# Hash attention with a feed-forward block: key tiles in groups of two, queries and keys turned by VectorE, hashes on column halves of TensorE

## The chip, the cores and the metric

One core of a Trainium2 chip. The metric is the device time of one execution in microseconds (us), lower is better. All runs are of one core; the runs of one kernel in one job mostly agree within 0.3%. Engines are named as the profile does: PE is TensorE (PEld its weight loads), DVE VectorE, ACT ScalarE, POOL GpSimd, SP the queue that issues the DMAs.

## The reference, cut to what matters

```python
batch, n_heads, seq, head_dim = (4, 8, 768, 64)        # proj: 64 x 6
q_bucket = sum((q @ proj > 0) * 2**arange(6))          # k_bucket likewise
mask     = q_bucket[..., :, None] == k_bucket[..., None, :]
scores   = where(mask, q @ k.T / 8, -1e9)
attn     = softmax(scores);  x = attn @ v              # -> (3072, 512)
h = x @ w_in;  g = h * sigmoid(1.702 * h)              # w_in 512 x 2048
out = g @ w_out                                        # w_out 2048 x 512
```

The two weights arrive as 64-bit floats and are converted to 32-bit on the chip, in 16 chunks each.

## The kernel before

Work goes by 16 pairs of heads. A pair has 12 units: six key tiles (`kt`) for each of two query halves (`c`). Per unit TensorE makes two score matrices (one per head, each on 64 rows of the array, f32, with a bf16 part that adds a huge negative number where the hashes differ), ACT takes the exponential, DVE sums, and TensorE multiplies with v (one head on each 64-column half of the array). The preparation of the next pair is put between the units:

```python
def turned(c, ...):                         # 2 per tensor: three transposes on TensorE, copy on ACT
    for i in range(HT):
        nc.tensor.transpose(tp[:, i, :], x[:, c * HT + i]..., ident)
    nc.scalar.mul(xt[:, cols], tp, ...)

def hashed(c, ...):                         # 2 per tensor: a matmul on the whole array
    nc.tensor.matmul(dots, pb, xt[:, cols], start=True, stop=True)
    nc.vector.tensor_scalar(bits[:, cols], dots, ...)

def scores(n, c, kt):
    for a, m, last in ((kb, qb, False), (kT, qT, True)):        # bf16 first, then f32
        for j in range(2):
            nc.tensor.matmul(ps[:, j, 0:HS], a[hs, keys], m[hs, cols], start=not last, stop=last)
    nc.scalar.activation(es[c][:, kt, :, 0:HS], ps[:, :, 0:HS], Act.Exp)
# ... in the loop over units u:
    scores(*units[u]); sums(*units[u - 1]); values(*units[u - 2])   # plus total, invert, norm at a half's end
    todo.pop(0)()                                                   # one step of the next pair's preparation
```

In the feed-forward, `hidden(n)` makes 16 strips of h for 512 tokens (8 matmul passes each), `outputs(n)` the result. Inside the first 16 strips w_out is converted, a chunk per strip, with one set of buffers:

```python
    nc.scalar.activation(g[:, fc, :], h, Act.Gelu_apprx_sigmoid)
    if convs:
        for _ in convert(*convs.pop(0)):    # sign, bits, xor, sign, (ACT) size, scale, (POOL) add, scale
            pass
```

## Time and profile before

| | before |
|---|---|
| median of 3 runs | 1122.27 us (1120.23 to 1122.54) |
| span of the profiled run | 1120.4 us |
| attention, to the first feed-forward matmul | 448.2 us |
| one pair of heads in the steady part | 27.10 us |
| first feed-forward matmul to first output matmul (two `hidden`) | 116.4 us |
| all output matmuls and the other `hidden`, from first to last start | 548.9 us |

The pair is the distance between the first f32 score matmul of the second pair (42.09 us) and of the last (421.53), over 14. The profile's lines that carry the argument are in the prediction. Two habits are needed to read them. PE is "busy" for 98% of the span, but its recorded spans overlap where matmuls are pipelined, so what a matmul takes of the array is the distance from start to start. And an f32 matmul is recorded as two passes: "x4" of an f32 matmul are two instructions, one per head, of two passes.

### The profile page before, as it was taken

The page shows a single profiled execution, that of the slowest core. Times are in us where ns is not written, and L with a number is a line of the kernel's source. Part 1 is how long each engine was busy: PE and PEld are TensorE (multiplying, and loading weights), DVE is VectorE, ACT ScalarE, POOL GpSimd, SP SyncE. Part 2 cuts the span into 40 slices and gives each one's busy share as a digit, 9 for nine tenths or more (in the row PEclk, how much of TensorE's full clock was granted, in tenths as well). Part 3 has the DMA queues.
Part 4 walks back from the last instruction along what each step waited for, and adds up shares of the span by engine and source line. Part 5 has one row for each costly group of instructions (what it writes and reads, how often), then busy time and mean ns, then how long its engine had stood idle before and what let it go on. Part 6 is the DMA issues. An engine that isn't in the chain of part 4 may idle for free.

```text
span 1120.4 us, 9656 instructions
## 1 busy us (share of the span) xinstructions
PE 1099.1 (98%) x3905; PEld 451.1 (40%) x3905; DVE 368.3 (33%) x646; ACT 290.0 (26%) x450; POOL 51.1 (5%) x40
## 2 busy tenths in 40 slices
PE   6999999999999999998999999999999999999997
PEld 3333333333333333443444444444444444444443
DVE  2666666666666667565000000000000000000000
ACT  3555555445445554322100110011001100110000
POOL 0000000000100000222000000000000000000000
PEclk9999999999999999999999999999999999999999
DMA  5222222222222220231000000000000000000000
GB/s 122 62 62 61 62 62 62 61 62 62 64 68 72 62 61 20 93 114 57 1 9 19 9 1 9 19 9 1 9 19 9 1 19 19 0 1 19 19 19 21
DMA packets 83541, 42.65 MB, mean 38 GB/s; under 512 B 76320, under 2 KB 76320, under 8 KB 83488
## 3 DMA queue, kind: packets, MB, share of 16 engines
q1 hardware_dynamic: 83488, 41.96, 13.8%
q8 instruction: 32, 0.52, 0.2%
q14 instruction: 21, 0.17, 0.1%
HBM read 35.65 MB, written 6.29 MB: 37 GB/s over the span
## 4 chain that ended last, share of the span: by engine, by line
PE 92%; DVE 4%; POOL 2%; issue 1%; DMA 1%; ACT 0%; SPq 0%; ACTq 0%; DVEq 0%
PE y L411 29%; PE h L399 24%; PE ps L216 16%; PE av L236 14%; PE hash L172 5%; PE tp L165 3%; PE dn L243 2%; POOL w_out_sb L127 2%; DVE bits L118 1%; DVE w_out_sb L125 1%; DMA k<-in_k_dram 1%; DVE sign L121 1%; DVE sign L115 1%; DVE bits L116 0%; ACT L401 0%
## 5 line engine op out<-in xcount | busy, mean ns | idle before, releaser
L399 PE MATMUL h<-xT,w_in_sb 128*128 128x512 f32 x768 | 333.1, 595 | 4.2 <-ACT g L401 3.8
L411 PE MATMUL y<-w_out_sb,g 128*128 128x512 f32 x768 | 330.4, 592 | 0.0
L399 PEld LDWEIGHTS h<-xT,w_in_sb 128*128 128x128 f32 x768 | 146.1, 191 | 189.9 <-issue 181.4
L411 PEld LDWEIGHTS y<-w_out_sb,g 128*128 128x128 f32 x768 | 145.9, 190 | 183.7 <-issue 183.7
L414 DVE COPY o<-y 128x512 f32<-128x512 f32 x24 | 16.6, 693 | 571.5 <-PE y L411 571.5
L217 ACT ACTIVATE e<-ps 128x768 f32<-128x768 f32 x192 | 155.6, 810 | 173.5 <-PE ps L216 171.6
L401 ACT ACTIVATE g<-h 128x512 f32<-128x512 f32 x96 | 56.9, 596 | 439.8 <-PE h L399 439.8
L236 PE MATMUL av<-e,v 128*64 128x385 f32 x768 | 166.9, 514 | 0.0
L216 PE MATMUL ps<-qT,kT 64*128 64x384 f32 x768 | 155.8, 484 | 0.0
L229 DVE TENSOR_TENSOR acc<-acc,e 128x768 f32<-128x768 f32 x128 | 122.2, 954 | 15.6 <-ACT e L217 12.3
L236 PEld LDWEIGHTS av<-e,v 128*64 128x64 f32 x768 | 38.2, 135 | 104.7 <-issue 104.6
L216 PEld LDWEIGHTS ps<-qT,kT 64*128 64x128 f32 x768 | 69.8, 191 | 0.2 <-issue 0.2
L216 PE MATMUL ps<-qb,kb 64*128 64x384 bf16 x384 | 64.7, 333 | 0.3 <-DVE qb L175 0.3
L216 PEld LDWEIGHTS <-kb 64*128 64x128 bf16 x384 | 18.5, 92 | 85.7 <-issue 85.6
L127 POOL TENSOR_TENSOR w_in_sb<-bits,w_in_sb 128x512 f32<-128x512 f32 x16 | 30.0, 1875 | 404.5 <-DVE w_in_sb L125 404.5
L225 DVE SCALAR_TENSOR_TENSOR acc<-e 128x768 f32<-128x768 f32 x32 | 30.6, 955 | 24.5 <-ACT e L217 24.5
L173 DVE TENSOR_SCALAR qb<-hash,q_off 128x384 bf16<-128x384 f32 x32 | 19.1, 598 | 55.7 <-PE hash L172 55.7
L173 DVE TENSOR_SCALAR kb<-hash,k_off 128x384 bf16<-128x384 f32 x32 | 19.8, 618 | 44.5 <-PE hash L172 44.5
L123 ACT ACTIVATE size<-raw 128x512 f32<-128x512 f32 x32 | 21.5, 672 | 43.8 <-DVE w_out_sb L130 43.8
L172 PE MATMUL hash<-kT,pb 128*128 128x384 f32 x64 | 30.3, 560 | 0.0
L172 PE MATMUL hash<-qT,pb 128*128 128x384 f32 x64 | 29.0, 537 | 0.0
L243 PE MATMUL dn<-acc,ones 128*64 128x384 f32 x128 | 26.1, 487 | 0.0
(49 smaller groups left out, 359.0 us busy)
## 6 DMA issues: line engine op xcount, KB each, us to landing
raw<-in_moe_w_in_dram SPq DMA_DIRECT2D x16, 512.0 KB, 3.6
raw<-in_moe_w_out_dram SPq DMA_DIRECT2D x16, 512.0 KB, 3.3
k<-in_k_dram SPq DMA_DIRECT2D x32, 192.0 KB, 3.2
q<-in_q_dram SPq DMA_DIRECT2D x32, 192.0 KB, 3.8
v<-in_v_dram SPq DMA_DIRECT2D x32, 192.0 KB, 3.2
out_dram<-o SPq DMA_DIRECT2D x24, 256.0 KB, 2.0
pb<-in_proj_dram SPq DMA_DIRECT2D x2, 1.5 KB, 2.2
```

What stands on the lines that cost most here:

```text
L127: nc.gpsimd.tensor_tensor(dst, bits.bitcast(F32), dst, op=Alu.add)
L165: nc.tensor.transpose(tp[:, i, :], x[:, c * HT + i].rearrange("p j d -> p (j d)"), ident)
L172: nc.tensor.matmul(dots, pb, xt[:, cols], start=True, stop=True)
L173: nc.vector.tensor_scalar(bits[:, cols], dots, 0.0, off[:, 0:1], op0=op, op1=Alu.subtract)
L216: nc.tensor.matmul(ps[:, j, 0:HS], a[hs, keys], m[hs, cols], start=not last, stop=last)
L217: nc.scalar.activation(es[c][:, kt, :, 0:HS], ps[:, :, 0:HS], Act.Exp)
L229: nc.vector.tensor_tensor(acc, acc, e[:, kt, :, 0:HS], op=Alu.add)
L236: nc.tensor.matmul(av[D * j : D * (j + 1), :], vt[:, kt, j, :], es[c][:, kt, j, :], start=(kt == 0), stop=(kt == T - 1))
L243: nc.tensor.matmul(dn[D * j : D * (j + 1), :], ones, acc[:, j, :], start=True, stop=True)
L399: nc.tensor.matmul(h, w_in_sb[:, kc, fc * P : (fc + 1) * P], xT[:, kc, n * NT : (n + 1) * NT], start=(kc == 0), stop=(kc == KC - 1))
L401: nc.scalar.activation(g[:, fc, :], h, Act.Gelu_apprx_sigmoid)
L411: nc.tensor.matmul(y, g[:, fc, i * P : (i + 1) * P], w_out_sb[:, fc, :], start=(fc == 0), stop=(fc == FC - 1))
```

## The change

The intent is to take work off TensorE, which sets attention's pace: the transposes go to DVE (the DMA brings q and k in blocks of 32 columns, which DVE turns block by block), the hash of a tensor is made in one step on the two column halves of the array, next to matmuls of the same shape, and the array changes between scores and values once per two key tiles. Some of DVE's sums go to POOL, and the conversion of w_out is spread over two strips per chunk. The diff, cut to its core:

```diff
+            def turn(n, name):
+                x = raws.pop((n, name))
+                xt = xts[n, name] = wk.tile([P, S], F32, ...)
+                nc.vector.transpose(xt, x.rearrange("p s i -> p (s i)"))
+            def hashed(n, name):
+                for c in range(2):
+                    nc.tensor.matmul(h[D * c : D * (c + 1), :], pf[name], xts[n, name][:, c * HS : (c + 1) * HS],
+                                     start=True, stop=True)
+            def featured(n, name):
+                nc.vector.tensor_scalar(f, dots.pop((n, name)), above[name][:, 0:1], FEAT[name], ...)
+                ...                       # four small DMAs bring f to its place, as operand of the scores
             def scores(n, c, kt):
-                for a, m, last in ((kb, qb, False), (kT, qT, True)):
+                for a, m, last in ((kT, qT, False), (kf, qf, True)):
...
-            def sums(n, c, kt):
+            def add(n, c, kts):
+                    if kt in (1, 3):
+                        nc.gpsimd.tensor_tensor(acc, e[:, kt - 1, ...], e[:, kt, ...], op=Alu.add)
+                    elif kt == 5:         # on DVE: tiles 4 and 5, then the two partial sums
...
+            for g in range(len(groups) + 3):
+                    for i in range(2):
+                        scores(n, c, kt + i)
...
+                    add(pn, pc, (pkt, pkt + 1))
+                    for i in range(2):
+                        values(pn, pc, pkt + i)
...
-                    if convs:
-                        for _ in convert(*convs.pop(0)):
-                            pass
+                    next(steps, None)     # a chunk in two strips, two sets of buffers, next load issued ahead
```

Left out: the constants of the hash, the loads and stores in the tokens' natural order, the second path for large inputs, which does not run here, and its threshold, and the scale of 1/8, which moves from the copies on ACT into the exponential.

More of the change, by code (lines that the diff above doesn't have):

```diff
@@ L24 @@
 BIT = 2.0**33
-SAFE, SAFE_BITS = 64.0, 0x42800000
+FEAT = {"q": 2.0**16, "k": -(2.0**16)}
+NORMAL = 2.0**-126
+SAFE, SAFE_BITS = 32.0, 0x42000000
 TINY = 2.0**-100
@@ L65 @@
     HS = HT * P
-    assert D == 64 and S == 2 * HS and HS < 512 and HP == KC and DM <= 512 and NB < 32
+    assert D == 64 and S == 2 * HS and HS < 512 and HP == KC and DM <= 512 and 2 * NB <= 32
     const = ctx.enter_context(tc.tile_pool(name="const", bufs=1))
@@ L91 @@
     k_off = offsets("k_off", -NB / 2.0)
+    pf, above = {}, {}
+    for x, signs in (("q", (1.0, -1.0)), ("k", (-1.0, 1.0))):
+        w = pf[x] = const.tile([P, D], F32, name=f"pf_{x}")
+        nc.vector.memset(w, 0.0)
+        th = above[x] = const.tile([P, 1], F32, name=f"above_{x}")
+        nc.vector.memset(th, 0.0)
+        for j in range(2):
+            rows = slice(D * j, D * (j + 1))
+            for i, sign in enumerate(signs):
+                c0 = 32 * j + NB * i
+                nc.vector.tensor_scalar(w[rows, c0 : c0 + NB], pb[rows, D * j : D * j + NB], sign, None, op0=Alu.mult)
+            for c in range(2):
+                r0 = D * c + 32 * j
+                nc.vector.memset(th[r0 : r0 + 2 * NB], 0.0 if signs[1] > 0 else -NORMAL)
+                nc.vector.memset(th[r0 : r0 + NB], 0.0 if signs[0] > 0 else -NORMAL)
     xT = const.tile([P, KC, N], F32, name="xT")
@@ L101, with convert @@
     CW = 512
-    cv = ctx.enter_context(tc.tile_pool(name="cv", bufs=1))
-    def convert(dst, src):
-        raw = cv.tile([P, CW, 2], U32, tag="raw", name="raw", bufs=2)
+    def convert(cv, dst, src):
+        raw = cv.tile([P, CW, 2], U32, tag="raw", name="raw")
         nc.sync.dma_start(out=raw, in_=src)
@@ L144, in load @@
             for j in range(2):
-                nc.sync.dma_start(out=x[:, :, j, :], in_=src[b, 2 * hp + j].rearrange("(p t) d -> p t d", p=P))
+                nc.sync.dma_start(out=x[:, :, j, :], in_=src[b, 2 * hp + j].rearrange("(t p) d -> p t d", p=P))
             tiles[name] = x
@@ L183, in attention @@
         with actx:
-            ld = actx.enter_context(tc.tile_pool(name="ld", bufs=2))
+            ld = actx.enter_context(tc.tile_pool(name="ld", bufs=1))
             wk = actx.enter_context(tc.tile_pool(name="wk", bufs=2))
             ep = actx.enter_context(tc.tile_pool(name="ep", bufs=1))
+            cv = actx.enter_context(tc.tile_pool(name="cv", bufs=1))
             st = actx.enter_context(tc.tile_pool(name="st", bufs=2))
@@ L195, in attention @@
                 nc.gpsimd.memset(e[:, :, :, HS : HS + 1], TINY)
-            tiles, ready = {}, {}
-            def fetch(n):
-                tiles[n] = load(ld, n)
-            def measure(n):
-                for i, name in enumerate("kq"):
-                    junk = st.tile([P, T, 2, D], BF16, tag="junk", name="junk", bufs=1)
-                    nc.scalar.activation(junk, tiles[n][name], Act.Square,
-                                         accum_out=sizes[:, 2 * n + i : 2 * n + i + 1])
+            feats = [{x: ep.tile([P, S], BF16, name=f"{x}f{i}") for x in "kq"} for i in range(2)]
@@ new lines, in attention, with fetch @@
+            for f in feats:
+                for x in "kq":
+                    nc.gpsimd.memset(f[x], 0.0)
+            raws, vts, xts = {}, {}, {}
+            def fetch(n, name):
+                b, hp = pairs[n]
+                x = raws[n, name] = ld.tile([P, S // 32, 32], F32, tag=name, name=name)
+                src = {"k": k, "q": q}[name]
+                for j in range(2):
+                    rows = src[b, 2 * hp + j].rearrange("(s p) (a i) -> a p s i", p=32, i=32)
+                    for a in range(D // 32):
+                        r0 = D * j + 32 * a
+                        nc.sync.dma_start(out=x[r0 : r0 + 32], in_=rows[a])
@@ new lines, in fetch_v @@
+            def fetch_v(n):
+                b, hp = pairs[n]
+                x = vts[n] = ld.tile([P, T, 2, D], F32, tag="v", name="v", bufs=2)
+                for j in range(2):
+                    nc.sync.dma_start(out=x[:, :, j, :], in_=v[b, 2 * hp + j].rearrange("(t p) d -> p t d", p=P))
+            def turn(n, name):
+                x = raws.pop((n, name))
+                xt = xts[n, name] = wk.tile([P, S], F32, tag=f"{name}T", name=f"{name}T")
+                nc.vector.transpose(xt, x.rearrange("p s i -> p (s i)"))
+                i = 2 * n + "kq".index(name)
+                junk = st.tile([P, S], BF16, tag="junk", name="junk", bufs=1)
+                nc.scalar.activation(junk, x.rearrange("p s i -> p (s i)"), Act.Square, accum_out=sizes[:, i : i + 1])
@@ new lines, in attention @@
+            dots = {}
+            def hashed(n, name):
+                h = dots[n, name] = mps.tile([P, HS], F32, tag="m", name="hash")
+                for c in range(2):
+                    nc.tensor.matmul(h[D * c : D * (c + 1), :], pf[name], xts[n, name][:, c * HS : (c + 1) * HS],
+                                     start=True, stop=True)
+            def featured(n, name):
+                f = wk.tile([P, HS], BF16, tag=f"{name}b", name=f"{name}b")
+                nc.vector.tensor_scalar(f, dots.pop((n, name)), above[name][:, 0:1], FEAT[name], op0=Alu.is_gt, op1=Alu.mult)
+                for j in range(2):
+                    for c in range(2):
+                        r0 = D * c + 32 * j
+                        nc.sync.dma_start(out=feats[n % 2][name][D * j : D * j + 32, c * HS : (c + 1) * HS],
+                                          in_=f[r0 : r0 + 32, :])
@@ L209, in scores @@
             def scores(n, c, kt):
-                (qT, qb), (kT, kb) = ready[n]["q"], ready[n]["k"]
+                qT, kT, qf, kf = xts[n, "q"], xts[n, "k"], feats[n % 2]["q"], feats[n % 2]["k"]
                 keys, cols = slice(kt * P, (kt + 1) * P), slice(c * HS, (c + 1) * HS)
                 ps = sps.tile([P, 2, 512], F32, tag="s", name="ps")
-                for a, m, last in ((kb, qb, False), (kT, qT, True)):
+                for a, m, last in ((kT, qT, False), (kf, qf, True)):
                     for j in range(2):
@@ L216, in scores @@
                         nc.tensor.matmul(ps[:, j, 0:HS], a[hs, keys], m[hs, cols], start=not last, stop=last)
-                nc.scalar.activation(es[c][:, kt, :, 0:HS], ps[:, :, 0:HS], Act.Exp)
+                nc.scalar.activation(es[c][:, kt, :, 0:HS], ps[:, :, 0:HS], Act.Exp, scale=1.0 / D**0.5)
             accs, avs = {}, {}
-            def sums(n, c, kt):
+            def add(n, c, kts):
                 e = es[c]
-                if kt == 1:
-                    acc = accs[n, c] = st.tile([P, 2, HS], F32, tag="acc", name="acc")
-                    nc.vector.scalar_tensor_tensor(acc, e[:, 0, :, 0:HS], T * TINY, e[:, 1, :, 0:HS],
-                                                   op0=Alu.add, op1=Alu.add)
-                elif kt > 1:
-                    acc = accs[n, c]
-                    nc.vector.tensor_tensor(acc, acc, e[:, kt, :, 0:HS], op=Alu.add)
+                for kt in kts:
+                    if kt in (1, 3):
+                        acc = accs[n, c, kt] = st.tile([P, 2, HS], F32, tag=f"acc{kt}", name=f"acc{kt}", bufs=1)
+                        nc.gpsimd.tensor_tensor(acc, e[:, kt - 1, :, 0:HS], e[:, kt, :, 0:HS], op=Alu.add)
+                    elif kt == 5:
+                        acc = accs[n, c, kt] = st.tile([P, 2, HS], F32, tag="acc", name="acc", bufs=1)
+                        nc.vector.scalar_tensor_tensor(acc, e[:, 4, :, 0:HS], T * TINY, e[:, 5, :, 0:HS],
+                                                       op0=Alu.add, op1=Alu.add)
+                        for o in (1, 3):
+                            nc.vector.tensor_tensor(acc, acc, accs.pop((n, c, o)), op=Alu.add)
             def values(n, c, kt):
@@ L233, in values @@
                     avs[n, c] = aps.tile([P, HS + 1], F32, tag="av", name="av")
-                av, vt = avs[n, c], tiles[n]["v"]
+                av, vt = avs[n, c], vts[n]
                 for j in range(2):
@@ L239, in total @@
             def total(n, c):
-                acc = accs.pop((n, c))
+                acc = accs.pop((n, c, 5))
                 dn = accs[n, c] = mps.tile([P, HS], F32, tag="m", name="dn")
@@ L263, in norm @@
                                                op0=Alu.add, op1=Alu.mult)
-            def steps_of(n):
-                ready[n] = {}
-                return prepare(wk, mps, tiles[n], 1.0 / D**0.5, ready[n]) + [lambda: measure(n)]
-            def whole(steps):
-                for _ in steps:
-                    pass
-            units = [(n, c, kt) for n in range(len(pairs)) for c in range(2) for kt in range(T)]
-            fetch(0)
-            for f in steps_of(0):
-                f()
@@ L277, in attention @@
-            todo, conv = [], iter(())
-            for u in range(len(units) + 4):
-                if u < len(units):
-                    n, c, kt = units[u]
-                    if (c, kt) == (0, 0):
-                        whole(conv)
-                        if n + 1 < len(pairs):
-                            fetch(n + 1)
-                            todo = steps_of(n + 1)
-                        conv = convert(*in_chunks[n])
-                        next(conv)
-                    scores(n, c, kt)
-                if 1 <= u <= len(units):
-                    sums(*units[u - 1])
-                if 2 <= u <= len(units) + 1:
-                    values(*units[u - 2])
-                    if units[u - 2][2] == T - 1:
-                        total(*units[u - 2][:2])
-                if 3 <= u <= len(units) + 2 and units[u - 3][2] == T - 1:
-                    invert(*units[u - 3][:2])
-                if 4 <= u and units[u - 4][2] == T - 1:
-                    norm(*units[u - 4][:2])
-                if u < len(units):
-                    if (c, kt) != (0, 0) and todo:
-                        todo.pop(0)()
-                    if 2 * c * T + kt >= 4:
-                        next(conv, None)
@@ L304, in attention, with step @@
-            whole(conv)
+            groups = [(n, c, kt) for n in range(len(pairs)) for c in range(2) for kt in range(0, T, 2)]
+            last = len(pairs) - 1
+            conv = [iter(())]
+            def step():
+                next(conv[0], None)
+            fetch(0, "k")
+            fetch(0, "q")
+            fetch_v(0)
+            for x in "kq":
+                turn(0, x)
+                hashed(0, x)
+                featured(0, x)
+                if last:
+                    fetch(1, x)
@@ new lines, in attention @@
+            for g in range(len(groups) + 3):
+                n, c, kt = groups[g] if g < len(groups) else (last + 1, 0, 0)
+                at = 3 * c + kt // 2
+                if n <= last:
+                    for i in range(2):
+                        scores(n, c, kt + i)
+                    if at == 0:
+                        for _ in conv[0]:
+                            pass
+                        conv[0] = convert(cv, *in_chunks[n])
+                        step()
+                    if n < last:
+                        if at == 0:
+                            turn(n + 1, "k")
+                        elif at == 1:
+                            turn(n + 1, "q")
+                if 1 <= g <= len(groups):
+                    pn, pc, pkt = groups[g - 1]
+                    add(pn, pc, (pkt, pkt + 1))
+                    for i in range(2):
+                        values(pn, pc, pkt + i)
+                if n < last and at in (1, 2):
+                    hashed(n + 1, "kq"[at - 1])
+                if 2 <= g <= len(groups) + 1 and groups[g - 2][2] == T - 2:
+                    total(*groups[g - 2][:2])
+                    invert(*groups[g - 2][:2])
+                if 3 <= g and groups[g - 3][2] == T - 2:
+                    norm(*groups[g - 3][:2])
+                if n < last:
+                    if at in (1, 2):
+                        x = "kq"[at - 1]
+                        featured(n + 1, x)
+                        if n + 2 <= last:
+                            fetch(n + 2, x)
+                    elif at == 3:
+                        fetch_v(n + 1)
+                if n <= last and at:
+                    step()
+                    if at >= 4:
+                        step()
@@ L306, in attention @@
+            for _ in conv[0]:
+                pass
             nc.vector.tensor_reduce(largest, sizes, axis=AX.X, op=Alu.max)
@@ L385, in feed_forward @@
         G = NT // P
-        outv = out.rearrange("(b p t) d -> b t p d", b=B, p=P)
-        convs = list(convs)
+        outv = out.rearrange("(b t p) d -> b t p d", b=B, p=P)
         with ExitStack() as fctx:
@@ L392, in feed_forward, with conversions @@
             gs = {}
+            def conversions():
+                todo = [convert(cv, *x) for x in convs]
+                for x in todo[:1]:
+                    next(x)
+                for i, x in enumerate(todo):
+                    for y in todo[i + 1 : i + 2]:
+                        next(y)
+                    for at, _ in enumerate(x):
+                        if at == 1:
+                            yield
+                    yield
+            if convs:
+                cv = fctx.enter_context(tc.tile_pool(name="cv2", bufs=2))
+            steps = conversions()
             def hidden(n):
@@ L401, in hidden @@
                     nc.scalar.activation(g[:, fc, :], h, Act.Gelu_apprx_sigmoid)
-                    if convs:
-                        for _ in convert(*convs.pop(0)):
-                            pass
+                    next(steps, None)
             def outputs(n):
```

## The prediction

> **What bounds the kernel now.** I read four views in this order: the page's first part, a table of stretches, the order of time on TensorE in the steady part, and the chain that ended last around the start of the second half.
>
> The page and the table of stretches (columns: stretch; busy us and instruction count of PE, weight loads, DVE, ACT, POOL; granted clock; DMA share; GB/s):
>
> ```profile
> PE 1099.1 (98%) x3905; PEld 451.1 (40%) x3905; DVE 368.3 (33%) x646; ACT 290.0 (26%) x450; POOL 51.1 (5%) x40
> ...
> 28.00:434.00 406.00, 406.00 (x2226) 146.40 (x2224) 282.42 (x484) 207.20 (x315) 28.73 (x15) 1.00 0.25 61
> ...
> 448.20:523.30 75.10, 71.26 (x161) 30.63 (x161) 48.86 (x93) 20.90 (x35) 18.99 (x15) 0.98 0.30 98
> 523.30:564.70 41.40, 41.40 (x97) 18.44 (x98) 1.96 (x4) 7.97 (x14) 1.27 (x1) 1.00 0.00 1
> ```
>
> There are two halves: attention to about 444.5 us, then 448.2 to 1114 the feed-forward. From 28 to 434 TensorE is busy every microsecond at full clock, with DVE at 70% and ACT at 51%. So TensorE sets attention's pace, but "busy" does not say that it computes: the recorded spans of pipelined matmuls overlap. What the array needs is seen from start to start. In the feed-forward the chain has 54.93 us for 128 matmuls of 512 columns, 429 ns each or 0.838 ns per column. An attention pass of 384 f32 columns should then take 0.322 us, and two half-array passes (two heads) run side by side in that time. The order of time on TensorE (start, us, line, what) shows what it takes:
>
> ```profile
> 201.11 0.34 PE L216 MATMUL ps<-qb,kb 64*128 64x384 bf16 x2
> 201.28 0.81 PE L216 MATMUL ps<-qT,kT 64*128 64x384 f32 x4
> 202.02 0.87 PE L236 MATMUL av<-e,v 128*64 128x385 f32 x4
> 202.82 0.34 PE L216 MATMUL ps<-qb,kb 64*128 64x384 bf16 x2
> ...
> 207.16 0.87 PE L236 MATMUL av<-e,v 128*64 128x385 f32 x4
> 207.85 0.81 PE L243 MATMUL dn<-acc,ones 128*64 128x384 f32 x4
> 208.60 0.55 PE L165 MATMUL tp<-ident,k 128*128 128x128 f32 x3
> 209.08 0.34 PE L216 MATMUL ps<-qb,kb 64*128 64x384 bf16 x2
> ...
> 212.18 0.87 PE L236 MATMUL av<-e,v 128*64 128x385 f32 x4
> 212.97 0.91 PE L172 MATMUL hash<-kT,pb 128*128 128x384 f32 x2
> 213.82 0.34 PE L216 MATMUL ps<-qb,kb 64*128 64x384 bf16 x2
> ```
>
> A unit (one key tile, one query half, two heads) takes 202.82 - 201.11 = 1.71 us, against 0.17 + 2x0.322 + 2x0.322 = 1.46 of streaming. It loses 0.25 at its two changes of shape: f32 scores (64 rows) to values (64 columns) take 0.74 instead of 0.644, values to bf16 scores 0.80 instead of 0.644. Values to dn (207.16 to 207.85), the same shape, take 0.69: the 0.05 inside the values stays, the 0.10 at their end is gone. A step of three transposes costs 209.08 - 208.60 = 0.48, a hash step 213.82 - 212.97 = 0.85 for 0.644 of streaming. Durations by line say what the rest is:
>
> ```profile
> L236 PE MATMUL av<-e,v x718: 487/537/538, 27.6 to 429.8; 128*64 128x385 f32 x180
> ...
> L172 PE MATMUL hash<-qT,pb x60: 486/538/590, 33.4 to 415.8; 128*128 128x384 f32 x60
> ```
>
> (min/median/max ns.) The first values matmul after a change lasts 50 ns more than the second, the first hash matmul 104 more: a first weight load that nothing hides, 64 columns in the one case, 128 in the other.
>
> In the feed-forward, PE does the whole y part without gaps. Only the start is slower: the chain that ended last runs through the conversion of w_out there, one conversion per 4.66 us:
>
> ```profile
> 510.73 1.28 POOL w_out_sb L127
> 513.43 0.70 DVE bits L118
> 514.62 0.70 DVE w_out_sb L125
> 515.39 1.28 POOL w_out_sb L127
> ```
>
> **What the Trainium skill says.** "TensorEngine Tiling (Array Packing)", Key Properties: changing the tiling mode, not just the tile, drains TensorE. The trace agrees: about 0.10 us at each change. "TensorE: Matmul & The Clock Gate", LDWEIGHTS (loading the stationary operand): a load takes the number of columns over 1.2, so 53 ns for 64 and 107 for 128. The trace agrees: 50 and 104 exposed. "SBUF — State Buffer", Who interferes with whom: a DVE instruction with two SBUF inputs, or in a 2-port mode, and a GpSimd instruction that reads SBUF exclude each other for a whole instruction. The trace agrees as far as it goes: POOL's 128x512 add takes 1.27 us alone and 1.92 where an accumulation of 0.95 on DVE is under way.
>
> ```profile
> L127 POOL TENSOR_TENSOR w_in_sb<-bits,w_in_sb x16: 1269/1915/1922, 35.9 to 434.5; 128x512 f32<-128x512 f32 x16
> ```
>
> "DMA: Bandwidth & Descriptors", Specifications: line rate needs pieces of at least 512 B. The q, k and v rows are 256 B already (76,320 packets under 512 B); the change makes q and k 128 B.
>
> **The change, part by part.** There are 16 pairs of heads with 12 units each.
>
> 1. Groups of two. Per group the array now does f32 scores, bf16, f32 scores, bf16, then both tiles' values. Cost: 4x0.322 + 2x0.165 for scores, 0.10 drain, 0.05 load, 4x0.322 for values, 0.10 drain. The order is turned too: f32 comes first after the change of shape, and its 128-column load of 0.107 is exposed, where the bf16 load hid it before. Sum 3.26, against 2x1.71 = 3.42. Gain 0.16 x 96 groups = 15 us, a half of what "half the switches" suggests.
> 2. Transposes leave TensorE: 64 steps x 0.48 = 31 us.
> 3. Hashes: 64 steps x 0.85 become 32 x 0.644, since both column halves run side by side and stand between values and dn, of the same shape, so no change is paid. 54.4 - 20.6 = 34 us.
> 4. The conversion of w_out is spread over two of the 3.43 us steps each (8 matmuls x 0.429) with two buffers, so its chain of 4.66 fits in 6.87. hidden(0) and hidden(1) should take 256 x 0.429 = 109.9 us; they took 448.2 to 564.7, so 6.6 us come back.
>
> Against it: (a) The start. Before, the first scores start at 13.2 and units stumble until about 21; by the steady rate attention starts effectively at 16. After, 8 smaller k and q loads, two transposes on DVE and 8 small feature DMAs go through one queue of some 0.65 us per issue: I count the q features landing at about 18, so 2 us later. (b) The end of attention: the last accumulation is three DVE operations (2.9 us) and not one, and values are a group behind: 2 us more before the feed-forward starts. Both are estimates from the issue and operation times in the trace.
>
> The steady pair: before 12x1.71 + 4x0.48 + 4x0.85 + 2x0.65 = 27.1; after 6x3.26 + 2x0.644 + 2x0.65 = 22.1. Is any other engine over 22.1? DVE: transposes 2x0.97 (estimate, from 0.58 for 384 columns), features 2x0.6, accumulation 6x0.955, inversions 2x1.39, norms 2x0.77, conversion 3.3: sum 16.5. POOL: 4 adds at about 1.9 (1.27 x 768/512) and one of 1.27: 8.9, some blocked. ACT: 12x0.81 + 2x1.03 + 0.66 = 12.4. DMA: in the stretch 28 to 400 it is 26.1% for 66,928 packets, 23 ns each on one of 16 engines; 8,192 packets per pair make 11.9 us, if a 128 B piece costs no more. None is over, and the new work is issued groups ahead of its use.
>
> Sum: 1122 - 15 - 31 - 34 - 7 + 2 + 2 = 1039. I take 1041, since small stalls are likelier than gifts.
>
> **The rivals.** (i) DVE becomes the bound. DVE and POOL exclude each other in 9.0 us of DVE's and 8.9 of POOL's work per pair; if five POOL operations each block DVE for 1 to 1.9 us, DVE has 21 to 26 us. For it: DVE waits in order for dn and hash, which makes it bursty. Against: in program order POOL's adds fall where DVE mostly does one-input work, and PE has about 2 to 3 us of slack before each dn. At 24 us a pair: 1072. (ii) Queue or DMA: 19 issues per pair in one in-order queue, 128 B pieces. v and the features are issued several us early. If pieces of 128 B cost double, DMA is at the bound: 1060 to 1080. I hold this unlikely. (iii) The hash buffer: q's hash needs k's feature read out of PSUM, which stands on DVE behind the inversion that waits for dn. I count about 0.9 us of slack; were it negative by 1 us, 15 us are lost: 1056. (iv) The exposed f32 load is hidden (issued while the array drains): 96 x 0.1 = 10 us better, 1030.
>
> **Range and chances.** All certain parts are on the engine that is the bound in every microsecond, so a gain is nearly sure; the spread comes from (i) to (iv). 1041, 8 in 10 in 1030 to 1062. Faster by over 2%: 0.97; within 2%: 0.02; slower: 0.01.
>
> **What would show it.** In the changed profile, from start to start: scores of a group 1.72 + 0.10, values 1.29 + 0.15, hash and dn 0.64 each, a pair 22.1 us; attention's last values near 369, feed-forward's start near 375, hidden(0) and hidden(1) 110 us, y unchanged at 54.93 per 128. DVE in attention near 75%, POOL near 45%. I am wrong if PE shows idle time behind DVE, POOL or a DMA in the steady part, if POOL's 128x768 add is much over 2 us or DVE's 0.955 grows, or if the f32 after values starts with no exposed load.

## The result, and the profile after

The changed kernel takes 1048.62 us (median of 4 runs, 1048.01 to 1049.67) against 1121.28 for the kernel before in the runs counted with it: ratio 0.9352, 95% interval 0.9336 to 0.9369. A ratio here is the mean time of one kernel's runs over that of the other's of the same rounds, so not quite the ratio of the medians. The prediction said 1041, in 1030 to 1062.

The page's first part and the table of stretches (columns as in the prediction):

```profile
PE 1020.6 (98%) x3713; PEld 441.2 (42%) x3713; DVE 361.5 (35%) x578; ACT 255.7 (24%) x386; POOL 164.8 (16%) x108
...
28.00:366.00 338.00, 338.00 (x2080) 140.49 (x2076) 275.03 (x392) 177.09 (x256) 135.09 (x76) 1.00 0.41 83
366.00:379.00 13.00, 6.28 (x38) 2.27 (x34) 9.87 (x17) 1.62 (x2) 2.78 (x2) 0.89 0.00 0
378.90:488.90 110.00, 109.98 (x252) 48.78 (x253) 50.26 (x95) 28.19 (x47) 19.15 (x16) 0.98 0.23 77
```

PE is still busy through the whole steady part, now with DVE at 81%, POOL at 40%, ACT at 52%. What is new is the second stretch: at attention's end PE has under half of 13 us, and the granted clock falls to 0.89. The order of time on PE in the steady part:

```profile
204.69 0.81 PE L256 MATMUL hash<-qT,pf_q 128*64 128x384 f32 x4
205.44 0.92 PE L275 MATMUL ps<-qT,kT 64*128 64x384 f32 x4
206.18 0.33 PE L275 MATMUL ps<-qf,kf 64*128 64x384 bf16 x2
...
207.25 1.52 PE L299 MATMUL av<-e,v 128*64 128x385 f32 x8
208.70 0.92 PE L275 MATMUL ps<-qT,kT 64*128 64x384 f32 x4
```

A group of two tiles takes 208.70 - 205.44 = 3.26 us, to the second digit what was worked out. The first f32 scores of a group have 0.92 in the record where the second have 0.81, and 0.74 from start to start where 0.644 would do: the exposed load. The hash has 0.75 here, of which 0.10 is the drain that would stand behind the values anyway.

Where the 74.3 us of the spans (1120.4 to 1046.1) came from, by starts in the two traces:

| piece | before | after | gain |
|---|---|---|---|
| first f32 scores of the second pair, at | 42.09 | 38.69 | 3.4 |
| 14 steady pairs | 14 x 27.10 | 14 x 22.15 | 69.4 |
| last pair and end of attention | 26.68 | 30.18 | -3.5 |
| two `hidden` with the conversion | 116.38 | 111.91 | 4.5 |
| from first output matmul to the end of the span | 555.8 | 555.3 | 0.6 |

The last pair has nothing left to prepare in either kernel, so the groups alone could gain there (6 x 0.16); that it loses 3.5 us is due to its end, which is worth a look. The starts are from one trace each, and scatter: experiments 2 and 10, with the same start, differ by 1.3 us there. In the order of time (all engines, weight loads left out; in square brackets the idle time before and what ended it):

```profile
369.80 1.54 POOL L286 TENSOR_TENSOR acc<-e 128x768 f32<-128x768 f32 x1
369.88 2.02 DVE L147 SCALAR_TENSOR_TENSOR w_in_sb<-size,w_in_sb 128x512 f32<-128x512 f32 x1 [0.66 <-POOL w_in_sb L144]
371.81 0.94 DVE L289 SCALAR_TENSOR_TENSOR acc<-e 128x768 f32<-128x768 f32 x1
372.79 2.02 DVE L292 TENSOR_TENSOR acc<-acc,acc 128x768 f32<-128x768 f32 x2
374.87 0.87 PE L306 MATMUL dn<-acc,ones 128*64 128x384 f32 x4 [3.90 <-DVE acc L292]
...
378.92 6.50 PE L497 MATMUL h<-xT,w_in_sb 128*128 128x512 f32 x10 [0.37 <-DVE largest L391]
```

The last step of the last conversion of w_in (L147) stands ahead of the last sums on DVE, and it takes 2.02 us because it begins 0.08 us after an addition on POOL and ends 0.5 after it. PE waits 3.90 us for the sums, and after that for the inversion. The ten first h passes then have 6.50 us; at 0.429 they would have 4.3. The first few take 0.85 from start to start, twice the usual, and the granted clock between 378.9 and 384 us is 0.61: it is not yet back (experiment 10).

### The profile page after: what moved, and what is told of

The parts are those of the page before. It is cut to its first block, busy times and chain, and to the rows that moved or that the text cites. A ratio compares the mean times of both kernels' runs of the same rounds, so it can differ in the third digit from the quotient of the medians.

```text
span 1046.1 us, 9494 instructions
## 1 busy us (share of the span) xinstructions
PE 1020.6 (98%) x3713; PEld 441.2 (42%) x3713; DVE 361.5 (35%) x578; ACT 255.7 (24%) x386; POOL 164.8 (16%) x108
## 4 chain that ended last, share of the span: by engine, by line
PE 97%; DVE 1%; SPq 1%; DMA 0%; issue 0%; POOL 0%; DVEq 0%
PE h L497 32%; PE y L507 32%; PE ps L275 17%; PE av L299 13%; PE hash L256 2%; PE dn L306 2%; SPq L265 0%; SPq L233 0%; DMA k<-in_k_dram 0%; DVE w_in_sb L147 0%; DVE acc L292 0%; DMA qf<-qb 0%; POOL w_in_sb L144 0%; DVE rt L313 0%; DVE rd L317 0%
## 5 line engine op out<-in xcount | busy, mean ns | idle before, releaser
L510 DVE COPY o<-y 128x512 f32<-128x512 f32 x24 | 16.6, 693 | 531.4 <-PE y L507 531.4
L275 PE MATMUL ps<-qT,kT 64*128 64x384 f32 x768 | 167.6, 514 | 0.0
L286 POOL TENSOR_TENSOR acc<-e 128x768 f32<-128x768 f32 x64 | 121.3, 1904 | 166.6 <-ACT size L140 92.8
L299 PE MATMUL av<-e,v 128*64 128x385 f32 x768 | 145.2, 499 | 0.0
L275 PE MATMUL ps<-qf,kf 64*128 64x384 bf16 x384 | 64.2, 324 | 3.5 <-DMA qf<-qb 3.5
L292 DVE TENSOR_TENSOR acc<-acc,acc 128x768 f32<-128x768 f32 x64 | 61.3, 958 | 5.6
L147 DVE SCALAR_TENSOR_TENSOR w_in_sb<-size,w_in_sb 128x512 f32<-128x512 f32 x16 | 32.3, 2016 | 10.6 <-POOL w_in_sb L144 10.6
L144 POOL TENSOR_TENSOR w_out_sb<-bits,w_out_sb 128x512 f32<-128x512 f32 x16 | 20.3, 1269 | 98.4 <-DVE w_out_sb L142 85.6
L138 DVE TENSOR_SCALAR sign<-bits 128x512 uint32<-128x512 uint32 x32 | 35.1, 1097 | 0.5
L275 PEld LDWEIGHTS <-kf 64*128 64x128 bf16 x384 | 19.7, 95 | 29.3 <-issue 5.0
L313 DVE STREAM_TRANSPOSE rt<-dn 128x384 f32<-128x384 f32 x32 | 18.7, 584 | 37.9 <-PE dn L306 37.9
L147 DVE SCALAR_TENSOR_TENSOR w_out_sb<-size,w_out_sb 128x512 f32<-128x512 f32 x16 | 11.1, 693 | 59.1 <-ACT size L140 59.1
```

The source lines that it names most:

```text
L138: nc.vector.tensor_scalar(sign, bits, 0xFF800000, None, op0=Alu.bitwise_and)
L147: nc.vector.scalar_tensor_tensor(dst, size, (1.125 * 2.0**-15) ** 2, dst, op0=Alu.is_ge, op1=Alu.mult)
L286: nc.gpsimd.tensor_tensor(acc, e[:, kt - 1, :, 0:HS], e[:, kt, :, 0:HS], op=Alu.add)
L292: nc.vector.tensor_tensor(acc, acc, accs.pop((n, c, o)), op=Alu.add)
L299: nc.tensor.matmul(av[D * j : D * (j + 1), :], vt[:, kt, j, :], es[c][:, kt, j, :], start=(kt == 0), stop=(kt == T - 1))
```

## The experiments

All kernels gave correct results. The medians of the kernel before were 1120.06, 1122.5, 1122.28 and 1120.55 us in the four jobs of the experiments, each on another chip, so a difference of 2 us between medians of different jobs says little. For small terms I use the pair (from the first f32 scores of the second pair to those of the last, over 14) and other starts in the traces. The main theory: in the steady part only TensorE's stream counts, made up of streamed columns, a drain of 0.10 us at each change of shape, and the first weight load behind it where nothing hides it.

**1. One key tile at a time.** Scores and values alternate again; all else as in the changed kernel.

```diff
                     for i in range(2):
                         scores(n, c, kt + i)
+                        if i == 0 and g >= 1:
+                            values(*groups[g - 1])
...
-                    for i in range(2):
+                    for i in range(1 if g < len(groups) else 0, 2):
                         values(pn, pc, pkt + i)
```

> The changed kernel with its score tiles and value tiles alternating again (one key tile, not two); all else as it is. Theory (every change of array shape costs its drain and the first weight load, and this order puts the 128-column f32 load first): 0.10 + 0.05 + 0.10 + 0.107 = 0.36 us more per two tiles, 95 times, 34 us: 1082 us. Rival A (only the drain and the values' load count, 0.25): 24 us, 1073. Rival B (the gain came from transposes and hashes alone, the grouping is worth nothing): 1049.

Measured: 1082.71 us, ratio 0.9667 (0.9649 to 0.9685); the pair 24.25 us. The order of time on PE:

```profile
203.43 0.92 PE L275 MATMUL ps<-qT,kT 64*128 64x384 f32 x4
...
204.44 0.87 PE L299 MATMUL av<-e,v 128*64 128x385 f32 x4
205.24 0.92 PE L275 MATMUL ps<-qT,kT 64*128 64x384 f32 x4
```

A unit takes 1.81 us, two of them 0.36 more than a group. Both rivals fall: the grouping is worth something, and the f32 load is part of the price of a change.

**2. The bf16 part first.** The old order inside a score tile, in groups of two.

```diff
-                for a, m, last in ((kT, qT, False), (kf, qf, True)):
+                for a, m, last in ((kf, qf, False), (kT, qT, True)):
```

> The changed kernel with the hash part (bf16) of each score tile ahead of the f32 part, as it was before the change; groups of two kept. Theory: the f32 weight load after the change of shape is hidden behind the bf16 matmuls, 0.10 us per group, 96 groups: 10 us faster, 1039 us, and a group takes 3.16 us from start to start for 3.26. Rival: the load is exposed to the array's drain in any order, or the order matters elsewhere (the features come by DMA): 1049 or slower.

Measured: 1041.15 us, ratio 0.9293 (0.9276 to 0.9310); the pair 21.58 us, 0.57 less than 22.15, or 0.094 per group.

```profile
212.31 0.34 PE L275 MATMUL ps<-qf,kf 64*128 64x384 bf16 x2
...
214.03 1.51 PE L299 MATMUL av<-e,v 128*64 128x385 f32 x8
215.48 0.34 PE L275 MATMUL ps<-qf,kf 64*128 64x384 bf16 x2
```

A group is at 3.17 us. The load was exposed by the order alone, and the changed kernel gives these 0.09 us away 96 times. The total gained 7.5 us by the medians and 6.3 by the two traced spans, not 10. In the traces the 14 steady pairs give 7.9, as worked out. The start loses: with f32 first, PE makes the f32 part of the first tile while q's features are still under way and then idles 3.49 us for them; with bf16 first it idles 5.03 us. From the first bf16 scores to the second pair's first f32 scores it takes 22.4 us for 21.0. So the expectation's rival, that the features come by DMA, holds for the first tile alone. The two `hidden` take 112.7 us for 111.9, and the last dn, at a low clock, 1.55 for 0.87 (experiment 10 takes that up).

**3. Both edits.** One tile at a time and bf16 first: the old order with the new preparation.

> Both of the last two: alternating tiles and bf16 first, which is the order of the kernel before, with the transposes and hashes of the changed one. Theory: two tiles take 2 x 1.71 = 3.42 us, as before the change, 0.16 more than the changed kernel's 3.26: 15 us slower, 1064 us. If grouping and order were independent by half the switches, 24 us: 1073.

Measured: 1065.24 us, ratio 0.9510 (0.9492 to 0.9528); the pair 23.11, 0.97 over the changed kernel's, which is 6 x 0.16. With experiments 1 and 2 this makes a square: grouping is worth 0.35 per two tiles with f32 first, 0.26 with bf16 first ((23.11 - 21.58) / 6). The two edits interact through the load.

**4. The hash on the whole array.** Two matmuls on 128 columns into the same sum; the weights of the other half are zero.

```diff
                 for c in range(2):
-                    nc.tensor.matmul(h[D * c : D * (c + 1), :], pf[name], xts[n, name][:, c * HS : (c + 1) * HS],
-                                     start=True, stop=True)
+                    nc.tensor.matmul(h, pf[name][:, D - D * c : 3 * D - D * c], xts[n, name][:, c * HS : (c + 1) * HS],
+                                     start=c == 0, stop=c == 1)
```

> The changed kernel with its two hash matmuls of a tensor on all 128 columns, one after the other (the other half of the weights is zero, so the result is the same). Theory: k's hash costs 0.644 of streaming more, 0.107 load, two drains of 0.10 and 0.05 load for the sums after it: 1.0 us; q's 0.644 + 0.107 + 0.10 = 0.85; 15 pairs: 28 us, and some 2 us at the start, 1078 us. Rival (only streamed columns count): 0.644 x 30 = 19 us, 1068.

Measured: 1077.41 us, ratio 0.9621 (0.9603 to 0.9640); the pair 23.98, 1.84 more, where 1.85 was expected and streamed columns alone make 1.29.

```profile
216.44 1.56 PE L257 MATMUL hash<-kT,pf_k 128*128 128x384 f32 x4
217.93 0.87 PE L307 MATMUL dn<-acc,ones 128*64 128x384 f32 x4
```

The hash takes 1.49 us here and 0.64 in the changed kernel where dn follows it there. So of the 1.84 us that this edit gives back, 0.55, about a third, come from the shape of the hash, which is that of its neighbours in the changed kernel, and the rest from streamed columns. (The cut leaves out the wider weights.)

**5. All sums on DVE.** This takes POOL out of the steady part, and tests the prediction's rival (i).

```diff
-                        nc.gpsimd.tensor_tensor(acc, e[:, kt - 1, :, 0:HS], e[:, kt, :, 0:HS], op=Alu.add)
+                        nc.vector.tensor_tensor(acc, e[:, kt - 1, :, 0:HS], e[:, kt, :, 0:HS], op=Alu.add)
```

> The changed kernel with the two partial sums of a query half on VectorE again, not on POOL. Theory (TensorE bounds the pair at 22.15 us and DVE has room): DVE's work is 16.5 + 4 x 0.955 = 20.3 us a pair without waits, the blocked operations (sign 1.77, last conversion step 2.02) go back to 0.42 and 0.69, the pair stays at 22.15; 1045 to 1051 us, a microsecond or two less at the end of attention. Rival (DVE is close to being the bound, as the prediction's rival i has it): 92% in bursts delays dn and hash, 1056 or more.

Measured: 1049.21 us, ratio 0.9350 (0.9337 to 0.9363): the same as the changed kernel; the pair 22.147 us in both. The last conversion step by line (min/median/max ns), first in the changed kernel, then here:

```profile
L147 DVE SCALAR_TENSOR_TENSOR w_in_sb<-size,w_in_sb x16: 2014/2015/2021, 39.0 to 369.9; 128x512 f32<-128x512 f32 x16
```

```profile
L147 DVE SCALAR_TENSOR_TENSOR w_in_sb<-size,w_in_sb x16: 691/692/694, 41.4 to 372.3; 128x512 f32<-128x512 f32 x16
```

The three-fold time of this operation was POOL's doing. It cost nothing in the steady part, and so sending sums to POOL gained nothing either. DVE is busy for 84% from 28 to 366 us here (285.0 of 338), for 81% with POOL's help. The microsecond or two expected at the end of attention did not come (last pair 30.04 us for 30.18): PE's wait for the last sums is 3.16 us for 3.90, but the dn behind it fell in a low clock and took 1.49 for 0.87.

**6. The old conversion of w_out.** One chunk inside each of the first 16 strips, one set of buffers.

```diff
-                    next(steps, None)
+                    if convs:
+                        for _ in convert(cv, *convs.pop(0), bufs=2):
+                            pass
```

> The changed kernel with w_out converted as before the change: one conversion inside each of the first 16 steps of the feed-forward, one set of buffers (two for the loaded data). Theory: the stretch from the feed-forward's first matmul to its first output matmul goes from 112.1 us to the 116.5 that it took before: 4.4 us slower, 1053. The prediction's number would be 6.6: 1055. Rival (the conversion was hidden in any case): 1049.

Measured: 1052.99 us, ratio 0.9393 (0.9378 to 0.9409), 4.4 us over the changed kernel. The two `hidden` take 116.8 us for 111.9. The spreading is worth 4 to 5 us, not 6.6. The starts of the passes show why. Here and in the kernel before, PE runs ahead of ACT for 17 strips and then waits for it at four strips running; apart from the slow first passes nothing else is lost. In the kernel before (waits of PE, 448 to 565 us):

```profile
PE h L399 <- ACT g L401: 3.8, 4, 1.0
```

From start to start these four strips cost 4.9 us in both kernels, and nothing in the changed one.

**7. The transposes alone.** The kernel before with q and k loaded in blocks and turned by DVE. With it come v and the result in the tokens' natural order and the scale of 1/8 in the exponential, since ACT's copies are gone; units, hashes and conversions are as before. The cut shows the turning alone.

```diff
             def turned(c, name=name, x=x, xt=xt):
+                if dve:
+                    if c == 0:
+                        nc.vector.transpose(xt, x.rearrange("p s i -> p (s i)"))
+                    return
```

> The kernel before with one part of the change alone: queries and keys are loaded in 32-column blocks and turned by VectorE; units, hashes and conversions as before. Theory: 60 transposing steps of 0.48 us leave the steady part (4 of 64 lie in the start): 29 us faster than before, 1092 us. As the prediction counted, 64 steps: 31 us, 1090. Rival (DVE, at 70% before, gets 1.94 us more per pair and delays TensorE): over 1100.

Measured: 1092.19 us for 1122.50, ratio 0.9731 (0.9716 to 0.9746): 30.3 us. By the total alone one can't choose between 60 steps and 64. The trace can: the pair goes from 27.10 to 25.19, by 1.91 = 4 x 0.48, and 15 pairs make 28.7; the second pair's first scores come 3.2 us earlier (38.93 for 42.09), a pair's 1.9 and 1.2 from the start. DVE, at 82% in the stretch from 100 to 300 us, delays nothing.

**8. A joined version that missed.** bf16 first; the second pair's loads issued behind the first pair's features; the conversion ended earlier in the last pair; the two partial sums added first, so that less follows the last exponential.

```diff
-                        nc.vector.scalar_tensor_tensor(acc, e[:, 4, ...], T * TINY, e[:, 5, ...], ...)
-                        for o in (1, 3):
-                            nc.vector.tensor_tensor(acc, acc, accs.pop((n, c, o)), op=Alu.add)
+                        nc.vector.scalar_tensor_tensor(acc, accs.pop((n, c, 1)), T * TINY, accs.pop((n, c, 3)), ...)
+                        for o in (4, 5):
+                            nc.vector.tensor_tensor(acc, acc, e[:, o, :, 0:HS], op=Alu.add)
...
-                if last:                  # inside the loop over k and q
-                    fetch(1, x)
+            if last:                      # behind it
+                for x in "kq":
+                    fetch(1, x)
...
-                    if at >= 4:
+                    if at >= 4 or n == last:
                         step()            # of the conversion
```

> A version meant to beat both: bf16 first; the second pair's loads behind the first pair's feature transfers; the two partial sums added first, so that only two DVE operations follow the last exponential, and the last conversion of w_in moved ahead of them. Theory: against bf16 first alone (1041.2) the start gains 1.9 us (the queue no longer issues four k loads before q's features), the end of attention 1.0 + 2.7: 1036 us. Rival (start and end are hidden or set by something else): 1041.

Measured: 1045.86 us, ratio 0.9321 (0.9306 to 0.9335): worse than bf16 first alone. The pair is at 22.19 and not at the 21.58 of bf16 first:

```profile
219.31 3.18 DVE L292 TENSOR_TENSOR acc<-acc,e 128x768 f32<-128x768 f32 x2
219.35 4.54 POOL L286 TENSOR_TENSOR acc<-e 128x768 f32<-128x768 f32 x2 [2.42 <-DVE acc L289]
...
222.54 0.87 PE L306 MATMUL dn<-acc,ones 128*64 128x384 f32 x4 [0.40 <-DVE acc L292]
```

Here is the prediction's rival (i) after all. The first DVE addition frees POOL's buffers (there is one of each), so POOL's next sum is let go just then, gets in between DVE's two remaining additions, and the second has to wait: 3.18 us for two that take 1.9. PE waits 0.40 for it, at one of the two dn of a pair (14 waits in 14 pairs); from the hash to dn it takes 1.21 from start to start where 0.64 would do, which is the 0.6 that the pair loses. In the changed kernel POOL's buffers come free only with DVE's last two additions, and the collision falls on operations that nobody waits for. This reading was an inference until the next two runs.

**9. The joined version without the new order of sums, and with it but without POOL.** The first (`e9`) keeps the changed kernel's sums; the second (`e10`) is the joined version with the edit of experiment 5.

> bf16 first, the second pair's loads behind the first pair's feature transfers, and the last conversion of w_in ended two groups earlier; the order of the sums as in the changed kernel. Theory: the steady pair stays without TensorE waits at 21.55 us, the start gains 1.4 us on bf16 first alone (1041.2) and the end of attention 2.7: 1037 us. Rival (the joined version lost its 5 us to the start or to the moved conversion, not to the order of the sums): 1041 or more.

> The joined version that missed (partial sums added first), with all sums on VectorE and none on POOL. Theory (dn waited because POOL's next partial sum got in between two of DVE's additions and shut the second out): without POOL the additions take 0.95 us each, dn does not wait, the pair is at 21.55 us and the time at about 1037. Rival (the order of the sums on DVE itself is late, or DVE at 94% is the bound): 1043 or more.

Measured: 1037.24 us, ratio 0.9247 (0.9234 to 0.9259), pair 21.58; and 1038.66 us, ratio 0.9255 (0.9240 to 0.9269), pair 21.58 too. By line, DVE's last additions in the joined version, and in the same without POOL's sums:

```profile
L292 DVE TENSOR_TENSOR acc<-acc,e x64: 957/1398/2115, 29.7 to 371.5; 128x768 f32<-128x768 f32 x64
```

```profile
L292 DVE TENSOR_TENSOR acc<-acc,e x64: 957/958/1832, 30.8 to 363.7; 128x768 f32<-128x768 f32 x64
```

The same order of sums is harmless without POOL, and POOL is harmless with the other order. It is the two together that cost 7 to 9 us. The start and the end are real gains: first f32 scores of the second pair at 38.49 for 39.85 (37.7 to 38.9 in the four traces with this start, 39.85 and 41.10 in the two of bf16 first without it), last pair to the feed-forward 27.2 for 30.2.

**10. Unread matmuls in the idle time.** bf16 first, with 22 pairs of bf16 matmuls ahead of the last dn and 14 behind it; nobody reads their result.

```diff
+                    if g == len(groups) + 1:
+                        busy(22)
                     total(*groups[g - 2][:2])
+                    if g == len(groups) + 1:
+                        busy(14)
```

> bf16 first, with 36 pairs of bf16 matmuls whose result nobody reads put into TensorE's idle time between the last values and the feed-forward (22 pairs ahead of the last dn, 14 behind). Theory: the clock that is granted stays full, the last dn takes 0.87 for 1.55 us and the stretch from the first feed-forward matmul to the first output matmul 110 for 112 us: about 2.7 us faster than 1041.2, 1038.5. Rival (the 112 has another cause): 1041 or a little slower.

Measured: 1039.12 us, ratio 0.9261 (0.9248 to 0.9273), against 0.9293 of bf16 first. From the chain that ended last (start, us, what), bf16 first and then this kernel:

```profile
367.45 1.57 PE dn L306 x4
...
372.18 112.86 PE h L497 x256
```

```profile
368.69 0.87 PE dn L306 x4
...
372.55 110.13 PE h L509 x256
```

The same 256 passes take 2.7 us less behind a TensorE that was kept busy, 110.13 for a streaming time of 109.9. The stretches in which they begin, bf16 first and then this kernel (columns as before; the share behind the engines is the granted clock):

```profile
372.20:378.00 5.80, 5.80 (x7) 2.48 (x8) 2.58 (x5) 0.00 (x0) 0.53 (x1) 0.53 0.49 181
```

```profile
372.50:378.00 5.50, 5.45 (x13) 2.58 (x14) 1.14 (x3) 1.59 (x2) 0.00 (x0) 1.00 0.57 194
```

All of the loss lies in the first passes, at about half the clock. In the changed kernel too: its first ten passes take 6.34 us from start to start where 4.29 would do, and the other 246 lose nothing. So the conversion no longer slows the two `hidden` there, only the clock does. The gain of the whole is 2.0 to 3.6 us by medians and ratios.

**11. All that worked.** bf16 first, the start and end of `e9`, and 9 + 14 pairs of unread matmuls.

> bf16 first, the reordered start and end, and 23 pairs of unread matmuls in the idle time before the feed-forward (9 ahead of the last dn, 14 behind). Theory (the gains of start and end and that of the clock are independent): 1037.2 - 2.4 = 1035 us, the first two hidden stretches 110.1 us. Rival (they overlap): 1037.

Measured: 1034.80 us, ratio 0.9228 (0.9214 to 0.9242): 14 us better than the changed kernel. The two `hidden` take 110.0 us.

## Why the prediction was right, and where its sizes were off

The measured 1048.6 lies in the range, and the direction and mechanism held: TensorE stayed the bound, and its stream became shorter by the parts named. By its steps:

1. Groups of two: 15 us. Right: 3.26 us per group, and putting the old order back costs 16.6 us (experiment 3). That the gain is half of what the count of changes suggests, since f32 first exposes its load, is shown by experiments 1 and 2.
2. Transposes: 31 us. The size of a step was right (1.91 us per pair, experiment 7), the count was not: only 15 of the 16 pairs are prepared in the steady part, so 60 steps or 28.7 us. The first pair's steps lie in the start, which the prediction had counted separately under (a).
3. Hashes: 34 us. The same slip: 60 steps of 0.85 less 30 of 0.644 are 31.7. The reasons for the step's size are shown by experiment 4. Terms 2 and 3 together were 4 us too large.
4. Conversion: 6.6 us. Measured 4.5 in the traces and 4.4 by undoing it. The term took all of the time over 109.9 for the conversion's. In the kernel before, 4.9 us were PE's four waits behind the conversion, and 1.6 us the low clock in the first ten passes; the changed kernel has none of the waits and loses 2.0 us to the clock (experiments 6 and 10).
5. Start: 2 us lost, measured 1.6 in one trace each (the second pair's scores less one pair: 14.98 and 16.54), less than the scatter allows to tell from 2.
6. End of attention: 2 us lost, measured 4.4 (last pair to feed-forward, less a pair without preparation: 4.9 and 9.3). The prediction counted DVE's three additions, and missed the conversion step in front of them, blocked by POOL for 1.3 us.

The terms together forecast a gain of 82.6 us (15 + 31 + 34 + 6.6 - 2 - 2); the traces show 74.3. Terms 2 and 3 (4 us), 6 (2.4) and 4 (2.1), less 0.4 of term 5, make 8.1 of the 8.3 us between. The large misses all point one way, so no luck of cancelling was in it; the 2 us added to the sum were too few for them, and the range had room. The steady pair, 22.1 predicted and 22.15 measured, was the part to rely on. Of the signs that the prediction named, DVE was at 81% for 75, POOL at 40% for 45, and the feed-forward began at 378.9 us for 375. POOL's add at 1.90 us and DVE's at 0.958 stayed as hoped; the exclusion fell on DVE operations that the list of signs did not name, 1.77 for 0.42 us (sign) and 2.02 for 0.69 (last conversion step).

Of the rivals, (i) did not come about in the changed kernel (experiment 5), but experiments 8 and 9 show that it was one reordering away. (ii) did not: DMA is busy for 41% in the steady part, and no wait of PE for features is on record there. (iii) did not show: PE has no waits there. (iv) is refuted as put (the load is exposed), though its 10 us could be had by changing the order. Not settled: how much of the difference between 7.5 us (medians) and 6.3 (traces) for bf16 first is scatter of the start and how much the chips of the two jobs.

## What to carry to other kernels

Where matmuls of different array shapes alternate, add up drains and first weight loads per change, and put behind a change the matmul that loses least there (here bf16 ahead of f32): it was worth about half as much here as the grouping. Count preparation steps by the iterations that hold them, not by all of them. Before moving work to POOL, look at which DVE operation it will stand beside: the same sums cost nothing or some 8 us, by the order of DVE's additions.

## What the Trainium skill lacked or had wrong

- "TensorEngine Tiling (Array Packing)", Key Properties, says that a change of tiling mode drains TensorE, and gives no size. Here a drain is about 0.10 us, and a pair of changes between 64-row scores and 64-column values costs 0.26 us with bf16 first and 0.35 with f32 first (experiments 1 to 3).
- "SBUF — State Buffer", Who interferes with whom, is right that the second of the two blocks fully, but not how it looks: the profile books the blocked time as busy time of the blocked instruction. A DVE step of 0.69 us reads 2.02, one of 0.96 up to 2.12, while the engine's idle time shows nothing.
- "DMA: Bandwidth & Descriptors", Specifications, has 512 B as the least size for line rate; the page has no measured time for a single piece of 128 or 256 B. By the packets' own records in the steady part, one of 256 B took 18 ns on its engine (before, 63,582 packets) and one of 128 B 13 ns (after, 79,872). So half the size cost 0.72 of the time (the prediction reckoned with the same time, its rival (ii) with double); the mean over all sizes fell from 23 to 18 ns, and the DMA share rose from 26% to 40% without harm.
- "TensorE: Matmul & The Clock Gate", Why this matters for your kernels, warns of idle gaps over about 3 us. That agrees in kind: with gaps of 4.0 and 2.4 us around one dn, the passes behind them took 2.7 us longer than without (experiment 10). But shorter gaps did it as well: in `e9`, with 1.63 and 2.44 us, the first ten passes took 6.83 us for 4.29. What the page lacks is that unread matmuls put into the gap recover the time inside a kernel.
